# Masks and identities by VectorE from one table, and another order and other banks for the second keys and for units 2 and 3

## The chip, the cores and the metric

The kernel runs on one core of a Trainium2 chip. The metric is device time in microseconds (us); the kernel before took 285.91 us, the median of three runs (285.8 to 287.22). A core has five engines with a queue of instructions each: TensorE (PE in the profile, its weight loads PEld), VectorE (DVE), ScalarE (ACT), GpSimd (POOL) and SyncE (SP). 16 DMA engines move data between HBM and SBUF. Here the loads of q, k, v and of the weights, which also turn float32 into 16-bit types, are issued by GpSimd; stores and DMA transposes are issued by SyncE.

## What is computed

Attention in a sliding window (each position sees those at most 32 away), and after it two matrix products with a GELU in between.

```python
batch, n_heads, seq, head_dim = 8, 8, 576, 64
scores = q @ k^T / sqrt(64)                    # per head, 576 x 576
scores = where(|i - j| <= 32, scores, -1e9)
attn = softmax(scores)
x = (attn @ v) -> (4608, 512)                  # tokens x (heads * head_dim)
h = x @ w_in                                   # 512 -> 2048
g = h * sigmoid(1.702 * h)
out = g @ w_out                                # 2048 -> 512
```

Inputs and output are float32; inside, q, k, v and the weights of attention are bfloat16, x, g and the weights float16, sums float32 in PSUM.

## The kernel before

**Units and tiles.** The 4608 tokens are cut into 36 units of 128 queries, and four units make a tile of 512 tokens (nine tiles). Queries are taken 32 rows late, so that the keys that the 128 queries of a unit need are the unit's own 128 keys and the first 64 of the next: two blocks of 64 queries against 128 keys each, for each of eight heads.

**One unit of attention.** `scores(u, tag)` makes the transposed scores of both blocks in two PSUM banks (48 matmuls for two units) and then ScalarE takes the exponential of each bank into `p` (L255, two a unit). `band(u)` (L263, VectorE) multiplies `p` by a mask of zeros and ones. `values(u, tag)` multiplies `p` by the values. For the first block they are the unit's 128 rows (`ve`), for the second the 128 rows that begin 64 later (`vo`), which `odd_v(u, eng, parts)` puts together from two halves of `ve` (L209: one copy of 64x264 words for each part). Each value row has a one behind it, so the product also brings the sum of the weights. `norm(u)` (L292, L293, VectorE) divides by it into `x`. `x_T` and `x_T2` (L309, L321) transpose `x` of one or two units on TensorE against the identity `identh`, and a copy by VectorE or ScalarE (L67) writes it to `xT`, the form that the first product needs.

**The opening.** All orders are written out by hand, under a manual schedule: each engine runs its instructions in the order in which the code issues them, and waits on semaphores. `opening()` handles the first two tiles' attention and the first tile's layer 1:

- `load_first(c, part)` (L142) loads the first 576 keys and queries in two parts each: part 0 of k (320 rows) and q (256 rows), enough for units 0 and 1, and part 1 of each (256 rows), for units 2 and 3. `T_first(c, part, tags, engs)` (L167) transposes them with `ident` on TensorE, in two PSUM banks, each of which one engine of `engs` copies out. `load_four` and `T_four` (L177, L188) do the same for the second tile's 512 keys and queries.
- GpSimd issues, in this order: k0, q0, (identity), v of units 0 to 2, w_in columns 0 to 511 (`load_w1(0)`, L115), (mask), k1, q1, (four cuts of the mask), w_in columns 512 to 1023, v 3, half of v 4, w_in columns 1024 to 1535, the other half of v 4, `load_four` of k and q, w_in columns 1536 to 2047, v 5 and 6, w_out rows 0 to 511 (`load_w2(0)`, L119), v 7 and 8, three more loads of w_out, and then k, q and v of later units. Eight semaphores serve these loads in turn, so that the issue of a load also waits for the landing of the load eight places ahead of it.
- `setup_mask` (L102, L105) fills the four blocks (64 columns each) of the mask on GpSimd with ones and cuts triangles by affine_select; `cut_mask` (L111) zeroes four quarters of the two blocks that serve where a window ends at a batch's end. `ident` comes from the library's `make_identity` (masks.py), a memset and an affine_select on GpSimd; `identh` is its cast to float16 (L588, VectorE).
- `keep_busy(n, tag, cols)` issues n matmuls of zeros into an unused bank (the "fillers": `junk` in the profile).
- `layer1_plain(t, d, half, tag)` makes two of the 16 feature blocks of layer 1 for half a tile (256 tokens) in one bank with eight matmuls; ScalarE's GELU (L389) reads it. Blocks d = 0, 1 need w_in columns 0 to 511, d = 2, 3 the next 512, d = 4, 5 the third, d = 6, 7 the fourth. GELU and exponential are in different tables of ScalarE, with an ACT_TABLE_LOAD between them.
- `do(self.l2, n)` takes the next n matmuls of the first tile's layer 2. They use w_out rows in order: the first 8 need its first load, the next 8 the second, the next 8 the third.

**Later tiles.** From the second tile on, both products are done with seven products for eight (the sums `a`, `b`, `xs`, `gs` on VectorE), and `front`, `back` and `l1_group` mix attention of the next tile with them. None of that is touched.

**Banks.** PSUM has eight banks here: `t` is two of them, and A, C, B, E, LA, LB one each.

Of the kernel before, what the change touches and what calls it, by code (L numbers as in the profile page):

```python
# [15 lines left out]
F32 = mybir.dt.float32  # L16
# [4 lines left out]
ALU = mybir.AluOpType  # L21

SQ = 64
# [3 lines left out]
class _Kernel:  # L27
# [69 lines left out]
        self.spark = cst.tile([128, 1], F32, name="spark")  # L97

    def setup_mask(self):
        pool, m = self.nc.gpsimd, self.mask  # L100
        lo, hi = slice(0, 64), slice(64, 128)
        pool.memset(m, 1.0)  # L102
        for blks, rows, sign in ((slice(0, 2), lo, 1), (slice(0, 2), hi, -1), (slice(2, 4), lo, -1), (slice(2, 4), hi, 1)):
            ap = m[rows, blks, :]
            pool.affine_select(out=ap, in_=ap, compare_op=ALU.is_ge, fill=0.0, base=0,  # L105
                               pattern=[[0, 2], [-sign, SQ]], channel_multiplier=sign)

    def cut_mask(self):
        lo, hi = slice(0, 64), slice(64, 128)
        for b, rows, cols in ((0, hi, slice(0, 32)), (0, lo, slice(32, 64)), (2, lo, slice(0, 32)), (2, hi, slice(32, 64))):  # L110
            self.nc.gpsimd.memset(self.mask[rows, b, cols], 0.0)  # L111

    def load_w1(self, c, n=1):
        w = 512 * n
# [446 lines left out]
    def opening(self):  # L561

        nc, dve, act, pool = self.nc, self.nc.vector, self.nc.scalar, self.nc.gpsimd
        self.setup()
        dve.memset(self.idle, 0.0)
        dve.memset(self.spark, 0.0)
        for t in self.ve:
            dve.memset(t[:, :, self.D:], 1.0)
        self.load_first("k", 0)
        self.load_first("q", 0)  # L570
        make_identity(nc, self.ident)
        act.activation(self.spark, self.spark, AF.Exp)
        for u in (0, 1, 2):
            self.load_v(u)
        self.load_w1(0)
        self.setup_mask()
        self.load_first("k", 1)
        self.load_first("q", 1)
        self.cut_mask()
        self.load_w1(1)  # L580
        self.load_v(3)
        self.load_v(4, slice(0, 1))
        self.load_w1(2)
        self.load_v(4, slice(1, 2))
        self.load_four("k")
        self.load_four("q")
        self.load_w1(3)
        dve.tensor_copy(self.identh, self.ident)  # L588
        self.keep_busy(10, "E", 512)
        self.T_first("k", 0, "AC", (dve, act))  # L590
        self.keep_busy(2, "E", 512)
        self.T_first("q", 0, ("LA", "LB"), (dve, act))
        self.keep_busy(1, "E", 512)
        for u in (5, 6):
            self.load_v(u)
        self.load_w2(0)
        for u in (7, 8):
            self.load_v(u)
        for c in (1, 2, 3):
            self.load_w2(c)  # L600
        self.load_kq("k", 8)
        self.scores(0, "t")
        self.scores(1, "AC")
        self.odd_v(0, dve)
        self.odd_v(1, dve)
        self.keep_busy(4, "E", 512)
        self.band(0)
        self.values(0, "t")
        self.band(1)
        self.norm(0)  # L610
        self.values(1, "AC")
        self.norm(1)
        self.keep_busy(2, "E", 512)
        self.x_T(0, "LA", act)
        self.keep_busy(1, "E", 512)
        self.x_T(1, "LB", act)
        self.T_first("k", 1, "AC", (dve, dve))
        h, n, gelus = [], [0], []

        def l1(half, *ds):  # L620
            for d in ds:
                self.layer1_plain(0, d, half, h[n[0] % len(h)])
                n[0] += 1

        self.layer1_plain(0, 0, 0, "B", gelus)
        self.T_first("q", 1, ("LA", "LB"), (dve, act))
        self.layer1_plain(0, 1, 0, "E", gelus)
        self.odd_v(2, dve)
        self.odd_v(3, dve, (0,))
        h[:] = ["B", "E", "LA", "LB"]  # L630
        self.scores(2, "t")
        self.scores(3, "AC")
        self.layer1_plain(0, 2, 0, "LA", gelus)
        self.layer1_plain(0, 3, 0, "LB", gelus)
        self.do(gelus)
        self.band(2)
        self.odd_v(3, dve, (1,))
        self.band(3)
        self.values(2, "t")
        self.norm(2)  # L640
        self.values(3, "AC")
        self.norm(3)
        l1(0, 4)
        self.x_T2(2, "A", dve)
        l1(0, 5)
        dve.tensor_copy(self.k_first, self.kT[0][:, :, 0:64])
        dve.tensor_copy(self.v_first, self.ve[0][0:64])
        for u in (8, 9, 10, 11):
            self.fetch(u)
        l1(1, 0, 1)  # L650
        halo = self.kT[4]
        self.T_four("k", "AC", (dve, dve))
        dve.tensor_copy(self.kT[4][:, :, 0:64], halo)
        l1(1, 2, 3)
        self.T_four("q", "AC", (dve, act))
        l1(1, 4, 5)
        self.odd_v(4, dve)
        self.scores(4, "t")
        self.scores(5, "AC")
        self.odd_v(5, dve)  # L660
        for i in (3, 1, 2, 4):
            self.w1_sums((i,), 0)
        self.odd_v(6, dve)
        self.odd_v(7, dve, (0,))
        for d, tag in ((6, "B"), (7, "E")):
            self.layer1_plain(0, d, 0, tag, gelus)
        self.do(self.l2, 3)
        self.scores(6, "t")
        self.do(self.l2, 3)
        self.scores(7, "AC")  # L670
        self.do(gelus)
        self.do(self.l2, 2)
        self.band(4)
        self.band(5)
        self.odd_v(7, dve, (1,))
        self.band(6)
        self.values(4, "t")
        self.norm(4)
        self.band(7)
        self.values(5, "AC")  # L680
        self.norm(5)
        self.do(self.l2, 8)
        self.values(6, "t")
        self.norm(6)
        self.do(self.l2, 2)
        self.values(7, "AC")
        self.norm(7)
        h[:] = "BE"
        n[0] = 0
        self.w1_sums((3,), 1)  # L690
        l1(1, 6, 7)
        self.x_T2(4, "A", act)
        self.do(self.l2, 2)
        self.x_T2(6, "t", dve)
        self.do(self.l2, 4)
# [216 lines left out]
```

## Time and profile before

| | |
|---|---|
| median of three runs | 285.91 us (285.8 to 287.22) |
| profiled execution | 285.75 us, of which the span is 284.0 us |
| PE busy | 272.8 us (96%), 3684 matmuls |
| DVE busy | 217.2 us (76%), 501 instructions |
| ACT busy | 193.9 us (68%), 340 instructions |
| POOL busy | 126.9 us (45%), 192 instructions |
| chain that ended last | PE 82%, DMA 7%, DVE 5%, POOL 4% |
| queue of GpSimd's loads | 106000 packets, 18.42 MB |
| granted TensorE clock | 1.0 |

The span is cut from the first instruction to the last; the times of runs have 1.75 us around it. Busy times of matmuls overlap, as they are pipelined, so a busy share of PE near 100% doesn't say that it is at its peak. The chain is followed back from the last instruction, at each step to what released it. The opening, to which the change belongs, lasts until about 47 us of the span; in the first 42 us TensorE is busy in a smaller share than later.

### The profile page before, as it was taken

The numbers are of one execution on the slowest core, as the hardware profiler recorded it, in microseconds if no ns is written. First come the engines' busy times: TensorE is split into PE (matmuls) and PEld (weight loads), VectorE is DVE, ScalarE is ACT, GpSimd is POOL, SyncE is SP. The second block draws the span as 40 slices with busy tenths as digits, with TensorE's granted clock in tenths as the row PEclk, the third lists the DMA queues.
The fourth block names the chain that finished last, engine by engine and source line by source line (L and its number), as shares of the span: only waits on it lengthen the run. The fifth ranks groups of instructions, "written<-read, shape, count | busy, mean of one in ns | idle before, by whom it ended". The sixth has DMA issues, their size and how long they took to land.

```text
span 284.0 us, 8953 instructions
## 1 busy us (share of the span) xinstructions
PE 272.8 (96%) x3684; PEld 223.3 (79%) x3684; DVE 217.2 (76%) x501; ACT 193.9 (68%) x340; POOL 126.9 (45%) x192
## 2 busy tenths in 40 slices
PE   6787999999999998999999999999999999999995
PEld 2466847776778887888888888888888888888884
DVE  1754997898887877798879887878788878946731
ACT  2556684799886778667966796689658875568411
POOL 8975446898599726739083909340110000000000
PEclk9999999999999999999999999999999999999999
DMA  8999999999999999999999999995422030201024
GB/s 90 182 193 196 184 204 159 193 124 147 136 154 152 200 127 195 124 203 143 201 102 189 131 203 82 198 146 140 132 58 71 26 113 14 81 2 74 2 95 133
DMA packets 149610, 37.63 MB, mean 132 GB/s; under 512 B 138048, under 2 KB 145216, under 8 KB 149568
## 3 DMA queue, kind: packets, MB, share of 16 engines
q0 software_dynamic: 106000, 18.42, 95.0%
q1 hardware_dynamic: 43120, 18.10, 34.2%
q8 instruction: 29, 0.48, 0.7%
q10 hardware_dynamic: 448, 0.52, 0.6%
q14 instruction: 13, 0.11, 0.1%
HBM read 36.83 MB, written 9.44 MB: 163 GB/s over the span
## 4 chain that ended last, share of the span: by engine, by line
PE 82%; DMA 7%; DVE 5%; POOL 4%; issue 1%; ACT 0%; DVEq 0%; POOLq 0%
PE o L70 37%; PE h L70 36%; PE pv L70 4%; DMA w<-in_moe_w_in_dram 4%; DMA xT<-x 3%; PE sc L70 3%; POOL ve L198 1%; POOL kq L142 1%; DVE xs L353 1%; DVE vo L209 1%; PE tp L321 1%; PE tp L231 1%; DVE a L334 1%; PE tp L188 1%; POOL w L115 1%
## 5 line engine op out<-in xcount | busy, mean ns | idle before, releaser
L418 ACT ACTIVATE g<-h 128x512 f16<-128x512 f32 x128 | 72.2, 598 | 35.7 <-PE h L70 34.9
L70 PEld LDWEIGHTS <-g 128*128 128x128 f16 x576 | 54.4, 98 | 9.5
L70 PEld LDWEIGHTS <-a 128*128 128x128 f16 x512 | 49.1, 97 | 12.3 <-DVE xs L353 2.2
L70 PE MATMUL h<-xs,a 128*128 128x256 f16 x384 | 57.6, 272 | 0.9 <-DVE xs L353 0.7
L70 PE MATMUL o<-w,g 128*128 128x256 f16 (+1 forms) x320 | 55.5, 294 | 0.0
L70 PEld LDWEIGHTS <-w 128*128 128x128 f16 x512 | 48.9, 98 | 8.4 <-DMA w<-in_moe_w_in_dram 1.7
L70 PE MATMUL h<-xT,w 128*128 128x256 f16 x384 | 54.0, 273 | 1.4 <-DMA w<-in_moe_w_in_dram 1.4
L209 POOL COPY vo<-ve 64x264 int32<-64x264 int32 x55 | 25.5, 463 | 61.3 <-PE pv L70 59.0
L70 PEld LDWEIGHTS <-gs 128*128 128x128 f16 x384 | 36.8, 98 | 4.7
L255 ACT ACTIVATE p<-sc 128x512 bf16<-128x512 f32 x72 | 36.9, 620 | 2.6 <-PE sc L70 2.5
L70 PE MATMUL o<-b,gs 128*128 128x256 f16 x256 | 37.6, 273 | 0.0
L70 PE MATMUL o<-b,g 128*128 128x256 f16 x256 | 37.5, 273 | 0.0
L198 POOL DMA_DIRECT2D ve<-in_v_dram x40 | 34.4, 865 | 6.2 <-DMA qst<-in_q_dram 2.8
L431 DVE TENSOR_TENSOR h<-h,s 128x512 f32<-128x512 f32 x32 | 22.3, 698 | 17.8 <-PE h L70 17.5
L131 POOL DMA_DIRECT2D qst<-in_q_dram x35 | 28.1, 804 | 3.5 <-DMA w<-in_moe_w_out_dram 2.8
L67 ACT COPY h<-h 128x512 f32<-128x512 f32 x32 | 18.9, 589 | 15.5 <-PE h L70 15.1
L293 DVE TENSOR_TENSOR x<-pv,rec 128x256 f16<-128x256 f32 (+1 forms) x53 | 27.6, 520 | 1.8
L131 POOL DMA_DIRECT2D kst<-in_k_dram x31 | 26.4, 855 | 5.0 <-DMA ve<-in_v_dram 2.6
L437 DVE TENSOR_TENSOR h<-h,s 128x512 f32<-128x512 f32 x32 | 22.4, 700 | 4.6 <-PE h L70 3.9
L263 DVE TENSOR_TENSOR p<-p,mask 128x1024 bf16<-128x1024 bf16 x36 | 25.0, 698 | 0.8 <-ACT p L255 0.6
L67 ACT COPY s<-h 128x512 f32<-128x512 f32 x32 | 19.2, 599 | 2.0 <-PE h L70 0.7
L70 PE MATMUL h<-xs,w 128*128 128x256 f16 x128 | 19.2, 273 | 0.0
(83 smaller groups left out, 343.7 us busy)
## 6 DMA issues: line engine op xcount, KB each, us to landing
out_dram<-o_sb SPq DMA_DIRECT2D x33, 256.0 KB, 4.6
ve<-in_v_dram POOLq DMA_DIRECT2D x32, 128.0 KB, 6.6
kst<-in_k_dram POOLq DMA_DIRECT2D x25, 128.0 KB, 6.6
qst<-in_q_dram POOLq DMA_DIRECT2D x21, 128.0 KB, 6.1
w<-in_moe_w_in_dram POOLq DMA_DIRECT2D x4, 512.0 KB, 8.9
w<-in_moe_w_out_dram POOLq DMA_DIRECT2D x4, 512.0 KB, 12.6
qst<-in_q_dram POOLq DMA_DIRECT2D x7, 96.0 KB, 6.4
kq<-in_q_dram POOLq DMA_DIRECT2D x2, 256.0 KB, 5.9
```

Of the source, the lines that this page charges most:

```text
L67: (eng.copy if eng is self.nc.scalar else eng.tensor_copy)(out, in_)
L70: self.nc.tensor.matmul(out, lhsT, rhs, start=start, stop=stop, skip_group_check=True)
L115: self.nc.gpsimd.dma_start(self.w1[:, :, c * 512:c * 512 + w], self.w_in[:, c * 512:c * 512 + w].rearrange("(k p) f -> p k f", p=128))
L131: self.nc.gpsimd.dma_start(t[off:off + n], src[b, :, s:s + n, :].rearrange("h s d -> s h d"))
L198: self.nc.gpsimd.dma_start(t[off:off + n, :, :self.D], self.v[b, :, s:s + n, :].rearrange("h s d -> s h d"))
L209: eng.tensor_copy(*((words(vo[64:128]), words(self.ve[u % 9][64:128])), (words(vo[0:64]), words(nxt)))[i])
L255: self.nc.scalar.activation(p[:, eo].rearrange("k h s -> k (h s)"), sc[eo], AF.Exp, scale=self.scale)
L263: (eng or self.nc.vector).tensor_mul(pv, pv, msk.to_broadcast([128, 8, 2, SQ]))
L293: dve.tensor_mul(x[:, 4 * at:4 * (at + n), :].rearrange("p (b h) d -> p b h d", b=n), acc[:, :, :, :D], r.to_broadcast([128, n, 4, D]))
L418: act.activation(g[:, f, 256 * half:256 * half + 256], bank.rearrange("p (i n) -> p i n", i=2), AF.Gelu_apprx_sigmoid)
L431: dve.tensor_add(e, b, s7)
L437: dve.tensor_add(c, b, s7)
```

## The change

The mask and both identities are made in another way. GpSimd writes one table D of 128x128 float32 with D[p, j] = p - j (iota). VectorE compares it with zero: D = 0 is `ident`, which it casts to `identh`; D >= 0 and D <= 0 on the two 64-row halves are the mask's triangles. The four cuts are VectorE's memsets. `setup_mask` and `cut_mask` are called right behind the first two loads, and GpSimd's queue goes from the table straight to v of unit 0. The order of the loads among each other stays as it was.

The second part of the keys (`T_first("k", 1)`) is transposed ahead of `x_T(0)` and `x_T(1)` and not behind them, with two fillers less, in LA and LB in place of A and C; its copies are by ScalarE and VectorE and not both by VectorE. `x_T(0)` uses bank t, `x_T(1)` LA, and the second queries B and E. Scores of units 2 and 3 follow at once (t, B and E), and the first two blocks of layer 1 come behind them, in A and C. On VectorE `band(2)` stands ahead of the second half of `odd_v(2)`, and on TensorE `values(2)` stands ahead of the third block of layer 1 and `values(3)` ahead of the fourth. The transposes of x of units 2 and 3 (`x_T2(2)`) come ahead of layer 1's fifth block and not behind it, in bank t. The banks of the blocks behind them follow from that.

```diff
@@ -97,18 +97,23 @@
         self.spark = cst.tile([128, 1], F32, name="spark")
 
     def setup_mask(self):
-        pool, m = self.nc.gpsimd, self.mask
-        lo, hi = slice(0, 64), slice(64, 128)
-        pool.memset(m, 1.0)
-        for blks, rows, sign in ((slice(0, 2), lo, 1), (slice(0, 2), hi, -1), (slice(2, 4), lo, -1), (slice(2, 4), hi, 1)):
-            ap = m[rows, blks, :]
-            pool.affine_select(out=ap, in_=ap, compare_op=ALU.is_ge, fill=0.0, base=0,
-                               pattern=[[0, 2], [-sign, SQ]], channel_multiplier=sign)
+
+        D = self.work.tile([128, 128], F32, name="gap", tag="s7", bufs=2)
+        self.nc.gpsimd.iota(D, pattern=[[-1, 128]], base=0, channel_multiplier=1,
+                            allow_small_or_imprecise_dtypes=True)
+        dve = self.nc.vector
+        dve.tensor_single_scalar(self.ident, D, 0.0, op=ALU.is_equal)
+        dve.tensor_copy(self.identh, self.ident)
+        for r in (slice(0, 64), slice(64, 128)):
+            d = D[r, r].rearrange("p (b s) -> p b s", b=1).to_broadcast([64, 2, SQ])
+            up = int(r.start > 0)
+            for blk, op in ((2 * up, ALU.is_ge), (2 - 2 * up, ALU.is_le)):
+                dve.tensor_single_scalar(self.mask[r, blk:blk + 2, :], d, 0.0, op=op)
 
     def cut_mask(self):
         lo, hi = slice(0, 64), slice(64, 128)
         for b, rows, cols in ((0, hi, slice(0, 32)), (0, lo, slice(32, 64)), (2, lo, slice(0, 32)), (2, hi, slice(32, 64))):
-            self.nc.gpsimd.memset(self.mask[rows, b, cols], 0.0)
+            self.nc.vector.memset(self.mask[rows, b, cols], 0.0)
 
     def load_w1(self, c, n=1):
         w = 512 * n
@@ -568,15 +573,14 @@
             dve.memset(t[:, :, self.D:], 1.0)
         self.load_first("k", 0)
         self.load_first("q", 0)
-        make_identity(nc, self.ident)
+        self.setup_mask()
+        self.cut_mask()
         act.activation(self.spark, self.spark, AF.Exp)
         for u in (0, 1, 2):
             self.load_v(u)
         self.load_w1(0)
-        self.setup_mask()
         self.load_first("k", 1)
         self.load_first("q", 1)
-        self.cut_mask()
         self.load_w1(1)
         self.load_v(3)
         self.load_v(4, slice(0, 1))
@@ -585,7 +589,6 @@
         self.load_four("k")
         self.load_four("q")
         self.load_w1(3)
-        dve.tensor_copy(self.identh, self.ident)
         self.keep_busy(10, "E", 512)
         self.T_first("k", 0, "AC", (dve, act))
         self.keep_busy(2, "E", 512)
@@ -610,11 +613,12 @@
         self.norm(0)
         self.values(1, "AC")
         self.norm(1)
-        self.keep_busy(2, "E", 512)
-        self.x_T(0, "LA", act)
+        self.T_first("k", 1, ("LA", "LB"), (act, dve))
         self.keep_busy(1, "E", 512)
-        self.x_T(1, "LB", act)
-        self.T_first("k", 1, "AC", (dve, dve))
+        self.x_T(0, "t", act)
+        self.keep_busy(1, "E", 512)
+        self.x_T(1, "LA", act)
+        self.T_first("q", 1, "BE", (dve, act))
         h, n, gelus = [], [0], []
 
         def l1(half, *ds):
@@ -622,26 +626,25 @@
                 self.layer1_plain(0, d, half, h[n[0] % len(h)])
                 n[0] += 1
 
-        self.layer1_plain(0, 0, 0, "B", gelus)
-        self.T_first("q", 1, ("LA", "LB"), (dve, act))
-        self.layer1_plain(0, 1, 0, "E", gelus)
-        self.odd_v(2, dve)
-        self.odd_v(3, dve, (0,))
-        h[:] = ["B", "E", "LA", "LB"]
         self.scores(2, "t")
-        self.scores(3, "AC")
+        self.scores(3, "BE")
+        self.layer1_plain(0, 0, 0, "A", gelus)
+        self.layer1_plain(0, 1, 0, "C", gelus)
+        self.odd_v(2, dve, (0,))
+        self.band(2)
+        self.odd_v(2, dve, (1,))
+        self.odd_v(3, dve)
+        self.values(2, "t")
         self.layer1_plain(0, 2, 0, "LA", gelus)
+        self.band(3)
+        self.norm(2)
+        self.values(3, "BE")
         self.layer1_plain(0, 3, 0, "LB", gelus)
         self.do(gelus)
-        self.band(2)
-        self.odd_v(3, dve, (1,))
-        self.band(3)
-        self.values(2, "t")
-        self.norm(2)
-        self.values(3, "AC")
         self.norm(3)
+        h[:] = ["A", "C", "LA", "LB", "B", "E"]
+        self.x_T2(2, "t", dve)
         l1(0, 4)
-        self.x_T2(2, "A", dve)
         l1(0, 5)
         dve.tensor_copy(self.k_first, self.kT[0][:, :, 0:64])
         dve.tensor_copy(self.v_first, self.ve[0][0:64])
@@ -653,6 +656,7 @@
         dve.tensor_copy(self.kT[4][:, :, 0:64], halo)
         l1(1, 2, 3)
         self.T_four("q", "AC", (dve, act))
+        h[:], n[0] = ["LA", "LB"], 0
         l1(1, 4, 5)
         self.odd_v(4, dve)
         self.scores(4, "t")
```

## The prediction

> **What bounds the kernel now.** I read four views. The first is the chain that ended last, in order of time (start us, length us, what); the edit touches only the first 30 us.
>
> ```profile
> 8.72 1.73 POOL kq L142 x2
> ...
> 13.27 10.13 DMA w<-in_moe_w_in_dram
> 23.44 1.05 PE h L70 x8
> 24.94 2.71 PE h L70 x24
> ...
> 38.17 1.30 DVE p L263 x2
> ...
> 39.97 1.83 PE o L70 x8
> 41.80 0.38 PE pv L70 x16
> 42.20 0.59 PE o L70 x2
> ```
>
> Up to 13.27 it names GpSimd's issues, then for 10.13 us a load of w_in (columns 1024 to 1535, call it C2), then TensorE, then VectorE's chain from 31.2 to 39.5, then TensorE. So the first question is whether C2 came late because it was issued late. The DMA view of the first 60 us (each cell 1.5 us) and three issues with KB and us from issue to landing answer that: first keys, C2, then the third w_out load (call it W2).
>
> ```profile
> DMA  0199999999999999999999999999999999999999
> GB/s 0 6 106 187 168 154 196 211 173 187 205 181 184 208 186 197 190 199 203 199 164 199 189 171 218 194 208 203 196 162 151 150 153 153 157 158 239 252 153 69
> ```
>
> ```profile
> kq<-in_k_dram POOLq DMA_DIRECT2D x1, 256.0 KB, 6.0
> w<-in_moe_w_in_dram POOLq DMA_DIRECT2D x1, 512.0 KB, 10.1
> w<-in_moe_w_out_dram POOLq DMA_DIRECT2D x1, 512.0 KB, 12.9
> ```
>
> The engines are never idle after 3 us. Ahead of and with C2, 3200 KB are queued; at the cells' 150 to 210 GB/s that is 16 to 22 us from 2.8 us on, and C2 landed at 13.27 + 10.1 = 23.4. It was waiting in a queue. The timeline (start, length) shows who waits:
>
> ```profile
> 12.41 0.60 PE L70 MATMUL junk<-idle 128*128 128x512 bf16 x2
> 14.75 0.64 PE L167 MATMUL tp<-ident,kq 128*64 128x128 bf16 x16 [0.50 <-DMA kq<-in_k_dram]
> 16.30 0.64 PE L167 MATMUL tp<-ident,kq 128*64 128x128 bf16 x16
> 17.85 0.70 PE L70 MATMUL sc<-kq 64*64 64x64 bf16 x48
> 23.44 1.05 PE L70 MATMUL h<-xT,w 128*128 128x256 f16 x8 [1.24 <-DMA w<-in_moe_w_in_dram]
> 24.33 0.61 PE L321 MATMUL tp<-identh,x 128*128 128x128 f16 x8
> 42.11 0.19 PEld L70 LDWEIGHTS <-g 128*128 128x128 f16 x2
> 42.20 0.59 PE L70 MATMUL o<-w,g 128*128 128x512 f16 x2
> ```
>
> TensorE idles 1.24 us for C2 at 23.44. The last pair matters most: at 42.11 the weights of the output product are loaded, at 42.20 its matmul starts; two us earlier (39.90) both started together. That matmul needs W2, issued at 29.28 (the timeline), landed 12.9 later, at 42.2. A second DMA bound stands there, hidden by 0.1 us.
>
> **Masks and identities.** GpSimd loses 0.22 + 0.29 (identity), 0.36 + 1.33 + 0.59 (mask): 2.79 us, and gains one table of indices. That row isn't there; the nearest are the memset (0.22) and the select (0.29) of the same shape; in 4-byte words up to twice that, so 0.2 to 0.6, and I take 0.3. The issues of the second keys and queries and all behind them come 1.9 (keys) to 2.5 us earlier. Nothing lands earlier, by the queue above: the issues only wait longer, and later ones wait for earlier landings anyway (1.56 and 2.07 us of idle ahead of w loads in GpSimd's timeline). Cost 0; if the queue were not the bound, up to -2.3 (a rival). VectorE gains the identity, its cast (already there, 0.20), four mask compares and four memsets: nearest rows 0.20 for 128x128, 0.28 to 0.66 for a 64x264 copy, 0.07 for its small memsets. 0.2 + 0.2 + 4 x 0.2 + 4 x 0.07 = 1.5, at most 3.4, from 3.6 us on. It sits idle until 6.60 (2.75 us, waiting for the first key transposes), so cover is there for 3.0; the identity is ready at 3.9 and first used at 6.01. Cost 0, 0.4 at the worst.
>
> **Second keys moved forward.** On TensorE the transposes of k part 1 now stand ahead of those of x0 and x1. They wait for their load, so TensorE idles from 12.4 to 14.75 (in before 14.25 to 14.75) with x0, x1 and fillers queued behind. Those take 2 x 0.23 (filler, two starts at 12.41 end 0.60 later, 0.38 each) + 2 x 0.23 (four starts 0.056 apart) = 0.9 and fit between 15.2 (the key transposes' last start) and 16.3, when the q part 1 transposes began because of their load. ScalarE's four copies between 15.2 and 17.58 (about 0.5 apart) fit as well; its copy of q then starts at 16.99 as before. Nobody else waits: x0, x1 are needed by layer 1 at 18 us. Cost 0; with one copy late, +0.5.
>
> **Scores 2 and 3 ahead of layer 1.** In before, eight layer-1 matmuls (16.88, 1.05 us) held TensorE when q's copies ended (DVE 17.46, ACT 17.58). Without them scores start at about 17.55, 0.3 earlier, and so does the second exponential (ends 19.43 in before, 19.13 then). VectorE follows: band(2) 0.61, three half copies of odd values 3 x 0.31, band(3) 0.61, norm(2) 0.20 + 0.61, norm(3) 1.17 (start to start, timeline at 20.2 to 23.6): 19.15 + 4.13 = 23.3. The load of values 3 ended a wait at 19.58 in before; now its copy follows band(2), at 19.76, and waits no more. TensorE has 32 layer-1 matmuls (0.11 apart, 3.5), two value products (0.45 each) in the same 18.05 to 22.6, so VectorE ends last. The transposes of x2 and x3 then end near 23.45, when C2 has just landed; in before they came behind its first eight matmuls. That takes 8 x 0.056 = 0.45 off TensorE's path, and 0.05 to 0.19 of a wait for their copy: k's second tile starts near 27.05 in place of 27.57. -0.5. Other end: every copy of values at 0.66 (the worst row, beside a GpSimd issue) is 3 x 0.37 = 1.1 later, +0.6. I take -0.5: 14 of the 16 up to 40 us are below 0.55.
>
> **What is late next.** From 31.2 to 39.5 VectorE's chain moves along by the 0.5; its loads of values (landed 31.95 to 37.04) still come in time. Then the product at 42.20 needs W2 at 42.2, and W2 does not move, since its queue has the same bytes in the same order. So at most 0.1 us gets past it. A loss of up to 0.6 would lose 0.1 there and pass with 0.5. Behind 42.2 TensorE is busy 17.77 of 17.80 us to 60, in an unchanged order.
>
> **Sum.** 0 (masks) - 0.5 (order) + 0.45 (given back at W2) = -0.05; ends -0.1 and +0.9. The profiled execution took 285.75 us (span 284.0, 1.75 around it); it becomes 285.7. The median of the three runs is 0.16 above it, so I predict 285.8.
>
> **Rival 1, slower: TensorE loses its clock in the new gap.** The first fillers ran at a slow rate: weight loads at 1.68, 2.10, 2.53 us, 0.43 apart, while the fillers at 12.41 are 0.22 apart. So there is a slow state at rest. In before, products and fillers never pause for over 1.9 us after 5 us (13.49 to 15.32); now, between 12.4 and 17.55, there are two fillers and transposes. It decides when the clock falls before layer 1 at 18 us and stays for half of its 32 matmuls or more: each then takes 0.11 more, +1.7 to +3.5, less 0.5 spare and 0.1: 286.9 to 288.6, likeliest 287.7. Against it: the gap alone is 2.35 us, and the clock reads 1.00 through all of before. The Trainium skill's page "TensorE: Matmul & The Clock Gate" (Why this matters for your kernels) wants no gap over about 3 us, by which the clock would stay; its Part 4 adds that transposes don't count as busy, which makes the gap 2.8 us up to the first filler at 15.2. No run here shows either yet. Chance 0.18, of which 0.15 beyond 0.5%.
>
> **Rival 2, faster: the issues were the bound.** The chain names GpSimd up to 13.27. If an engine ran dry between issues, C2 and W2 come up to 2.3 us earlier: 283.5. Against: no cell of the DMA row falls below 9. Chance 0.09, of which 0.07 beyond 0.5%.
>
> **Rival 3, slower: VectorE's new work and GpSimd's issues hinder each other.** Two value copies beside issues took 0.66 and 0.63 where 0.29 is usual. If the v issues at 3.6 to 6.2 are held for the length of eight VectorE operations, the stream runs dry once: +0.5 to +2, 286.3 to 287.8. Against: the v issue beside the cast took 0.901, its fellows 0.888 and 0.893. The Trainium skill, "SBUF — State Buffer" (SBUF: two separate sides), says a VectorE operation that takes the shared port blocks GpSimd's writing of descriptors; these three rows show no sign of it. Chance 0.07, 0.05 beyond.
>
> **Chances.** The forecast has 0.66, all within 0.5% (1.43 us, about what a measurement of this kernel can tell from no change). With the rivals' small ends: faster 0.07, same 0.73, slower 0.20. The range goes from 284.7 (a third of rival 2, and spread between runs) to 287.7 (rival 1's likeliest); it leaves out rival 2's larger part (0.07), rival 1 above (0.08) and rival 3's end (0.02).
>
> **What would show it.** Right: second keys and C2 land at 14.7 and 23.4 though issued about 2 us earlier; scores 2 near 17.55; the x2, x3 transposes ahead of C2's matmuls; k's second tile near 27.05; the W2 product again at 42.2. Wrong: layer-1 matmuls 0.2 apart or a granted clock below 1 between 14 and 22 us (rival 1); W2's matmul well before 42 (rival 2); lower GB/s in cells before 10 us (rival 3); value copies or exponentials later than listed, with the product past 42.5.

## Result and the profile after

The change made the kernel slower by a little: 287.34 us, the median of 15 runs (285.84 to 288.68), against 285.8 us for the kernel before in the same comparison; the ratio is 1.004, with a 95% interval of 1.0025 to 1.0055. This ratio, like all those below, compares the runs in the faster of two states in which a kernel runs here, and so is not the quotient of the two medians (1.0054). The profiled execution took 288.68 us, its span is 286.9 us and its mean granted clock 0.994 (before: 285.75, 284.0 and 1.0). It is the slowest of the 15, 1.34 us above their median, so it shows more loss than the kernel usually has. Times of one kernel spread by one to three us. Two things that differ between executions of the same instructions are seen below: where the steps of TensorE's clock fall, and when a group of DMA transposes at 107 to 113 us gets through. Whether they make up the whole spread isn't shown.

The first view is the timeline of TensorE in the kernel after (start us, length us, engine, line, operation, shapes, count, and in brackets the idle time before and who ended it):

```profile
14.62 0.71 PE L172 MATMUL tp<-ident,kq 128*64 128x128 bf16 x16 [2.06 <-DMA kq<-in_k_dram]
15.67 0.63 PE L314 MATMUL tp<-identh,x 128*128 128x128 f16 x4
17.09 1.07 PE L172 MATMUL tp<-ident,kq 128*64 128x128 bf16 x16
18.53 0.89 PE L70 MATMUL sc<-kq 64*64 64x64 bf16 x48 [0.37 <-DVE kq L67]
19.35 1.92 PE L70 MATMUL h<-xT,w 128*128 128x256 f16 x16
24.26 0.89 PE L326 MATMUL tp<-identh,x 128*128 128x128 f16 x8
28.57 1.11 PE L193 MATMUL tp<-ident,o_sb 128*64 128x128 bf16 x32
42.91 0.61 PE L70 MATMUL o<-w,g 128*128 128x512 f16 x2
```

TensorE idles 2.06 us ahead of the second keys, nearly as foreseen (2.35). What follows was not foreseen: the second queries' transposes take 1.07 us where they took 0.64, and scores 2 and 3 0.89 where they took 0.70. Scores 2 start at 18.53 (forecast 17.55), the second tile of keys at 28.57 (forecast 27.05), and the product that needs W2 at 42.91 (forecast 42.2). The table of engines by stretch (start and end, length, busy us of each engine with its count, then the granted clock; the last two columns, of the DMA, aren't used here) says why:

```profile
core 0: us, PE busy (x) PEld busy (x) DVE busy (x) ACT busy (x) POOL busy (x), PEclk, DMA share, GB/s
8.23:11.64 3.41, 1.78 (x57) 1.06 (x59) 2.90 (x7) 2.35 (x5) 3.41 (x6) 1.00 1.61 192
11.64:15.05 3.41, 1.20 (x48) 0.97 (x46) 2.32 (x7) 0.00 (x0) 1.63 (x3) 1.00 1.74 185
15.05:18.47 3.42, 3.11 (x34) 1.95 (x28) 1.38 (x2) 2.02 (x4) 1.35 (x2) 0.50 1.64 187
18.47:21.88 3.41, 3.09 (x78) 2.49 (x80) 1.82 (x5) 2.97 (x6) 2.55 (x3) 1.00 1.45 197
```

The clock's own record, kept with the trace, has it full from 4.81 us on, half for one stretch of 3.41 us, and full again. The stretch before the half one is the one with the gap: TensorE was busy 1.20 us of 3.41.

In the DMA view, k1, C2 and W2 (KB, us from issue to landing) read:

```profile
kq<-in_k_dram POOLq DMA_DIRECT2D x1, 256.0 KB, 8.0
w<-in_moe_w_in_dram POOLq DMA_DIRECT2D x1, 512.0 KB, 11.8
w<-in_moe_w_out_dram POOLq DMA_DIRECT2D x1, 512.0 KB, 12.8
```

They were issued at 6.62, 10.65 and 29.64 (before 8.67, 13.27 and 29.28) and landed at 14.6, 22.4 and 42.4 (before 14.7, 23.4 and 42.2). So 2.05 us of earlier issue brought the keys 0.1 us. C2 came one us earlier, which the prediction did not foresee. That the earlier issue did it isn't shown: in two kernels below whose issues stayed at the old times (before without its fillers, and the masks with GpSimd's old work) it landed at 22.37 and 22.52 too, and nothing in the change waits for it.

A second loss lies far behind the change. In the profiled execution after, ScalarE's exponentials and GELUs run 0.88 us later than before's up to 106 us, and 2.58 us later at 112. The waits of TensorE from 97 to 118 us (total, times, longest), and then the chain there:

```profile
PE sc L70 <- DMA kT<-kst: 1.2, 1, 1.2
PE h L70 <- DVE xs L358: 0.9, 1, 0.9
```

```profile
103.87 8.23 DMA xT<-x
...
113.80 1.05 PE h L70 x8
```

The same two views of before, the one wait and the transpose in the chain:

```profile
PE h L70 <- DVE xs L353: 0.7, 1, 0.7
100.79 8.72 DMA xT<-x
```

Before had only the second of the two waits there, and its chain goes through a DMA transpose of x at this place as well; in the change that one starts 3.08 us later.

### The profile page after: what moved, and what is told of

The parts are those of the page before. It is cut to its first block, busy times and chain, and to the rows that moved or that the text cites. A ratio compares the mean times of both kernels' runs of the same rounds, so it can differ in the third digit from the quotient of the medians.

```text
span 286.9 us, 8946 instructions
## 1 busy us (share of the span) xinstructions
PE 274.1 (96%) x3681; PEld 224.6 (78%) x3683; DVE 219.2 (76%) x509; ACT 194.7 (68%) x341; POOL 124.7 (43%) x182
## 4 chain that ended last, share of the span: by engine, by line
PE 83%; DVE 7%; DMA 6%; POOL 2%; issue 1%; ACT 1%; POOLq 0%; DVEq 0%
PE o L70 37%; PE h L70 36%; PE pv L70 4%; PE sc L70 3%; DMA xT<-x 3%; DMA kq<-in_k_dram 3%; DVE vo L214 1%; DVE a L339 1%; DVE xs L358 1%; DVE p L268 1%; POOL ve L203 1%; PE tp L326 1%; PE tp L236 1%; DVE x L298 1%; POOL kq L147 1%
## 5 line engine op out<-in xcount | busy, mean ns | idle before, releaser
L436 DVE TENSOR_TENSOR h<-h,s 128x512 f32<-128x512 f32 x32 | 22.4, 699 | 17.8 <-PE h L70 17.6
L442 DVE TENSOR_TENSOR h<-h,s 128x512 f32<-128x512 f32 x32 | 22.4, 699 | 4.6 <-PE h L70 4.0
```

The lines of the kernel that those rows point to most:

```text
L436: dve.tensor_add(e, b, s7)
L442: dve.tensor_add(c, b, s7)
```

## Experiments

Three theories were stated at first. A: the clock that TensorE loses because of the gap is the loss. B: the new order is slower by itself. C: the loss arises later, in DMA transposes behind the opening. "M", later on, is the suspicion that the new masks cost something. In three comparisons the kernel before took 286.23 (first four kernels), 286.47 (next four) and 286.11 us (last four).

**Fillers in the gap.**

```diff
+        self.keep_busy(9, "E", 512)
         self.T_first("k", 1, ("LA", "LB"), (act, dve))
```

> The changed kernel with nine fillers (0.22 us each, 2.0 us) ahead of the second keys' transposes, in the gap that ran from 12.4 to 14.6. Theory A (the clock drops to half because of the gap, and that is the loss): mean granted clock back to 1.00, layer-1 matmuls 0.11 apart everywhere, x2 and x3's transposes end near 23.5, and the time equals that of before within 0.3% (285.5 to 286.5). Theory B (the order itself is slower, by its waits on VectorE): clock 1.00 too, but the time stays near 287.3. Theory C (the loss arises in the later DMA transposes and has nothing to do with the opening): time stays near 287, with the opening as early as before.

286.1 us, ratio 1.0009 (0.999 to 1.0028). The clock was at 0.998 or more in 11 of 12 runs, where the change without fillers had 0.987 to 0.994 in 14 of 15. One line that adds work takes the loss away, so A holds for the median. The products of this kernel are in the order of the change, so B, as the cause of the loss, falls. The two intervals just touch here (1.0028 and 1.0025); with four fillers, below, they are apart.

**The order alone**, with the masks of before (`setup_mask`, `cut_mask` and `make_identity` at their old places).

> The changed order and banks, with masks and identities made by GpSimd as before. Theory A: the clock falls as in the changed kernel (mean 0.99) and the time is the changed kernel's within 0.2%, 286.8 to 287.8. A theory by which VectorE's mask work or the earlier issues cost the time expects before's 285.8 here.

287.74 us, ratio 1.0061 (1.0037 to 1.0084), with a clock of 0.987 to 0.994 in nine of ten runs. The slow part of the change is the order with its gap. The tenth run is the profiled one, whose clock came up only at 10.56 us and then stayed; it shows the opening as forecast (scores 2 at 17.40, k's second tile at 27.10).

**The masks alone**, with the old order.

> Masks and identities by VectorE from the table, with the order and banks of before. Theory A and the prediction's queue: loads issued about 2 us earlier land at the same times (second keys 14.7, columns 1024 to 1535 of w_in near 23), clock 1.00, time 285.8 within 0.2%. If the earlier issues help: 283.5 to 285.2. If VectorE's work beside GpSimd's issues hurts: over 286.5.

286.85 us, ratio 1.0028 (1.0006 to 1.005), and that with the clock at 0.994 to 1.0. This was not expected by A, and it falls where the expectation for VectorE hindering GpSimd's issues had it (over 286.5). The trace shows no sign of that mechanism, though: the issues of v take as long as before. In its profiled execution, the slowest of the 12, k1 landed at 15.34 (before 14.7). The time is lost at two places: the W2 product starts 0.36 us later than before's, and another 0.5 us goes at 107 to 113 us.

**The kernel before without the three fillers around x0 and x1.**

```diff
-        self.keep_busy(2, "E", 512)
         self.x_T(0, "LA", act)
-        self.keep_busy(1, "E", 512)
         self.x_T(1, "LB", act)
```

> The kernel before without the three fillers between the second value product and the second keys' transposes; nothing else is moved. Theory A with transposes not counting as work: the clock falls as in the changed kernel (mean 0.99), and the time rises by 0.7 to 1.7 us. Theory A with only an idle TensorE counting (its gaps here stay below 1.2 us): clock 1.00 and 285.8.

286.27 us, ratio 1.0013 (0.9995 to 1.0032). The clock fell in 11 of 12 runs. So before's fillers were holding its clock. The time rose less than the 0.7 to 1.7 us that were expected, by 0.4 us with an interval that reaches to nothing: a lost stretch there costs less than in the change. The profiled execution, one of three runs at 0.988 (two lost stretches), by stretch:

```profile
9.92:13.33 3.41, 1.71 (x38) 0.90 (x36) 3.20 (x9) 1.35 (x4) 3.32 (x9) 1.00 1.48 195
13.33:16.75 3.42, 2.95 (x26) 1.94 (x27) 1.82 (x5) 1.14 (x2) 3.35 (x5) 0.50 1.51 197
```

TensorE was busy for half of the first stretch, and the clock is half in the next.

**The order alone, with fillers** (nine, as above).

> The new order with the masks of before, and nine fillers of 512 columns ahead of the second key transposes, so that TensorE has no idle gap there. Theory A (the lost clock is the whole loss): the granted clock stays at 1.0 and the time is that of the same kernel with the new masks, 0.1% over before or less, 286.1 where before takes 286.2. Theory M (the masks cost 0.28% by themselves, as the run of the masks alone measured, and the order alone is worth the -0.5 us that was predicted): ratio about 0.998, 285.6. Theory B (the order itself is slower): 1.003 or more with the clock at 1.0.

The clock was at 0.997 or more in 11 of 12 runs, but the median is 287.15 us, ratio 1.0023 (1.0001 to 1.0046): neither A nor M foresaw that, and the interval holds the 1.003 of B. Five of its runs lie at 287.4 to 289.1 us with the clock at 0.997 or more; no trace shows why, so this run doesn't tell whether the order itself costs 0.2% with the old masks. The profiled execution (286.94 us) reaches the point forecast for the opening, and then gives it up. Its timeline of TensorE:

```profile
17.35 0.70 PE L70 MATMUL sc<-kq 64*64 64x64 bf16 x48 [0.57 <-DVE kq L67]
27.05 1.11 PE L188 MATMUL tp<-ident,o_sb 128*64 128x128 bf16 x32
42.02 0.59 PE L70 MATMUL o<-w,g 128*128 128x512 f16 x2 [0.30 <-DMA w<-in_moe_w_out_dram]
```

Scores 2 start 0.20 us ahead of the forecast, k's second tile at 27.05, the very number of it, and ScalarE's work is 0.52 us ahead of before from 32 to 41 us. Then TensorE waits 0.30 us for W2, and 0.19 us are left at 49. They go at 107 to 113 (0.2 lost) and at 210 to 215 us (0.4 lost).

**Transposes instead of an idle gap.**

```diff
+        tp = self.bank("E", [128, 4, 128], BF16, "tp")
+        for i in range(38):
+            nc.tensor.transpose(tp[:, i % 4, :], self.idle[:, 0:128], self.ident)
         self.T_first("k", 1, ("LA", "LB"), (act, dve))
```

> The changed kernel with 38 transposes of a zero tile (about 2.1 us) instead of an idle TensorE ahead of the second key transposes; the transposes write a bank that nobody reads. If any work of TensorE keeps its clock up (the profiled runs so far: the clock fell after stretches of 3.41 us with TensorE busy 0.35 and 0.50 of the time, transposes counted, and stayed after 0.52, 0.53 and 0.63): clock 0.998 to 1.0 and the time of the run with nine fillers, ratio 1.000 to 1.002. If transposes do not count as work for the clock: granted clock 0.987 to 0.994 in nearly all runs and 1.004, as the change without fillers.

The clock stayed at 0.998 or more in 11 of 12 runs; 286.46 us, ratio 1.0025 (0.9996 to 1.0053), a little outside the expected 1.000 to 1.002. Four runs at 287.8 to 289.3 widen the interval, three of them with the clock held, so the time settles nothing here and the clock does. By stretch:

```profile
10.90:14.31 3.41, 2.64 (x65) 2.48 (x66) 3.06 (x8) 0.21 (x1) 2.18 (x3) 1.00 1.65 187
14.31:17.73 3.42, 2.85 (x73) 2.15 (x74) 1.64 (x3) 2.19 (x4) 1.54 (x2) 1.00 1.47 196
```

Without the transposes, TensorE's products fill 0.26 and 0.29 of these two stretches, less than in the stretch without fillers in before (0.39, with transposes 0.50) after which the clock fell. So transposes count as work for the clock.

**Four fillers instead of nine.**

> The changed kernel with four fillers instead of nine. The idle gap shrinks from 2.2 to about 1.35 us, which lifts the least busy stretch of 3.41 us from 0.35 to about 0.60. Theory A with a limit near one half: the clock stays at 0.998 to 1.0 and the ratio is 1.000 to 1.002. If the clock wants a gap near nothing: 0.994 and 1.004, the order of 0.9 us slower than with nine fillers.

286.14 us, ratio 0.9994 (0.998 to 1.0008), clock at 0.998 or 1.0 in all 12 runs, though TensorE still idles 1.32 us ahead of the second keys. Its stretch with the transposes shows once more that these count, since products alone fill only 0.23 of it, as in the stretch of the change after which the clock fell:

```profile
13.64:17.05 3.41, 2.15 (x42) 1.60 (x42) 1.23 (x3) 1.51 (x3) 1.35 (x2) 1.00 1.46 200
```

About 0.85 us of work that nobody reads is worth 0.46% (1.3 us) against the change without it, by the two ratios to before.

**The masks alone, with GpSimd's old work kept** on a second mask that nobody reads, so that its issues are at the old times.

> The masks and identities by VectorE in the old order of work, and GpSimd still makes a second mask that nobody reads, at the old places, so that its issues of the second keys and of all behind them stay nearly at the times of before. If the 0.28% of the masks alone came from the earlier issues: ratio 1.000, within 0.1%. If it came from VectorE's work or from anything else that went with the masks: 1.003 again.

286.69 us, ratio 1.0018 (0.9999 to 1.0037): between the two expectations, and it settles neither. In its profiled execution the whole loss is there at 49 us: the W2 product starts 0.60 us late.

**The first two W2 products later**, on the version with four fillers.

```diff
         self.norm(6)
-        self.do(self.l2, 2)
         self.values(7, "AC")
...
         self.x_T2(4, "A", act)
-        self.do(self.l2, 2)
+        self.do(self.l2, 4)
```

> The changed kernel with four fillers, and its first two products with W2 moved behind the last layer-1 work of the opening, so that W2 may land some 3 us later. If W2 is what takes the gain back (the run with four fillers was 0.20 us ahead of before at 38 us and 0.01 at 49): 0.2 us ahead at 49 us and to the end of the profiled run, ratio 0.998 to 0.999. If the 0.2 is lost to something else at 41 to 49 us: 0.0 at 49 and 0.9994 again.

286.18 us, ratio 1.0014 (0.999 to 1.0037); no gain. ScalarE's work is 0.35 us ahead of before at 45 us, and 0.08 behind at 49. The chain shows VectorE's `norm` in W2's place: its last multiplication ends at 42.46, and the values of unit 7 start at 42.51. W2 landed at 41.8 in this execution, so two limits lie 0.6 us apart; the two products (0.44 us) had been filling part of the wait for the later one, and now take their time behind it.

**The late transposes of x by TensorE**, on the version with four fillers: `x_T2(14, "t", act)` within the second group's products, in place of two DMA transposes.

```diff
                 self.values(u + n - 1, "t")
                 self.norm(u + n - 1)
-                self.x_T(u + n - 1)
+                if n == 1:
+                    self.x_T(u + n - 1)
...
                 if t == 2 and n in (1, 3) and i == 7:
                     self.values(u + n, "t")
                     self.norm(u + n)
-                    self.x_T(u + n)
+                    if n == 1:
+                        self.x_T(u + n)
+                if t == 2 and n == 3 and i == 2:
+                    self.x_T2(u + n - 1, "t", self.nc.scalar)
```

> The changed kernel with four fillers, and the last two transposes of x for the fourth tile (units 14 and 15, about 98 to 112 us) made by TensorE with one copy by ScalarE instead of by two DMA transposes. Theory C (the second step at 107 to 113 us, +1.7 us in the profiled run of the change, +0.5 with the masks alone, -0.8 in another, comes from when these DMA transposes get through): no step of more than 0.2 us upwards at 106 to 112, some 0.5 us down, times closer together, ratio 0.996 to 0.998. If it comes from the DMA transposes of the keys beside them: TensorE still waits there in some runs, ratio 0.999 to 1.001 and a spread as before.

285.78 us (285.37 to 286.79), ratio 0.9991 (0.9974 to 1.0008). The chain at the place of the second loss:

```profile
101.10 0.45 PE tp L326 x8
...
106.54 0.63 PE sc L70 x32
107.17 1.57 PE o L70 x12
108.73 0.44 PE h L70 x4
```

There is no DMA and no wait in it. The transposes, at 101 us, cost 0.39 us, and 0.95 us come back by 118. Both waits, that for x and that for the keys' transposes, are gone with two DMA transposes fewer. One execution would not show it, since the one with transposes in the gap has no wait there either; but all three profiled executions with this edit (this one and the next two) have none, and ten of the eleven without it have one. So C is right about the place of the second loss. The median gains no more than the measurement can tell from nothing, and the times did not come closer together as expected: 1.42 us from lowest to highest, where the version with four fillers has 1.44.

**Both edits on the version with four fillers, and both on the kernel before.**

> Both edits together: 0.2 us and 0.5 us if both theories hold, ratio 0.995 to 0.998, 0.7 us below before. If the W2 edit brings nothing, as the one with the transposes alone.

> The kernel before with the same two edits, and none of the change. If the changed order is worth its 0.2 to 0.5 us once the clock is held and W2 is out of the way, this one is 0.1 to 0.2% slower than the version with both edits on the change: ratio 0.997 to 0.999, with a clock below 1 in about a quarter of the runs, as before. If it is as fast as that version, the change brought nothing even then.

285.97 us, ratio 0.9991 (0.9973 to 1.0008), and 286.15 us, ratio 1.0009 (0.9987 to 1.003). The second is 0.18% slower than the first, as expected, with three of its 12 runs at a clock of 0.994, also as expected, and the first is as fast as the version with the transposes alone, as expected if the W2 edit brings nothing. But the intervals cover these differences, and neither is at the 0.995 to 0.998 and 0.997 to 0.999 of the theories or beats the kernel before by more than the uncertainty. The second one's profiled execution is worth more than its time. It lost its clock at another place, that of before's 1.24 us wait for C2:

```profile
19.87:23.28 3.41, 1.58 (x39) 1.04 (x38) 3.28 (x10) 3.38 (x6) 1.56 (x2) 1.00 1.50 195
23.28:26.69 3.41, 3.41 (x21) 2.63 (x22) 0.90 (x3) 0.93 (x2) 2.33 (x3) 0.50 1.45 195
```

The kernel before has the same weak spot in its profiled execution, TensorE busy 1.82 us of 3.41:

```profile
21.31:24.72 3.41, 1.82 (x38) 1.52 (x33) 2.22 (x7) 2.66 (x6) 1.25 (x3) 1.00 1.54 193
```

Of its 103 runs in the three comparisons 19 show a clock below 0.995, though not where they lost it. In the first two comparisons the median of such runs lies 0.9 and 0.6 us above that of the others. The new order fills that wait with the transposes of x2 and x3.

How far ScalarE's exponentials and GELUs stand from before's in the profiled executions (us, minus is earlier), beside the start of the first W2 product (the kernels that move this product are left out):

| kernel | W2 product | at 38 us | at 49 | at 100 | at 112 | at 275 |
|---|---|---|---|---|---|---|
| the change | 42.91 | +1.00 | +0.73 | +0.88 | +2.58 | +2.72 |
| nine fillers | 42.06 | -0.20 | -0.15 | -0.14 | -0.13 | +0.01 |
| order alone | 41.95 | -0.47 | -0.26 | -0.25 | -0.33 | +0.03 |
| masks alone | 42.56 | -0.25 | +0.35 | +0.36 | +0.88 | +0.90 |
| before, no fillers | 43.20 | +1.29 | +1.06 | +1.07 | +1.25 | +1.26 |
| order alone, fillers | 42.02 | -0.52 | -0.19 | -0.18 | +0.05 | +0.41 |
| transposes in the gap | 42.04 | -0.22 | -0.07 | -0.06 | -0.85 | -0.70 |
| four fillers | 42.20 | -0.20 | -0.01 | -0.01 | -0.11 | +0.04 |
| masks, old issues | 42.80 | -0.01 | +0.59 | +0.60 | +0.64 | +0.63 |
| x by TensorE | 41.87 | -0.30 | -0.34 | -0.34 | -0.66 | -0.90 |

The first three columns of numbers tell the story of the opening (before's W2 product starts at 42.20): whatever was gained by 38 us, the shift at 49 is that of the W2 product, to 0.02 us in eight of the ten rows and to 0.09 in the other two (before without fillers, transposes in the gap). In seven rows that product started within 0.05 us of W2's landing. In the change it came 0.5 us after W2's landing at 42.4: VectorE released the values of unit 5 only at 40.20, and eight products and the values of unit 6 stood between these and the W2 product. The step at 112 does not follow from being late: before without fillers is 1.07 us late at 100 us, later than the change, and its step is 0.2 us.

## Why the prediction was wrong, step by step

**The step that failed is "Second keys moved forward".** It counted the idle time (12.4 to 14.75; measured 12.56 to 14.62) and who was queued behind it, and put its cost at 0, because everything fitted into the time. It priced the gap in work and not in clock. (The description of the change is off by one there: before has three fillers around x0 and x1 and the change two, so it has one less, and neither of the two stands in the gap.) The gap left 1.20 us of work in a stretch of 3.41, the next stretch ran at half clock, and the transposes of the second queries and the scores took 0.6 us more; with the waits between them, scores 2 came 1.0 us after the forecast. At 38 us the change is 1.2 us behind the same kernel with four fillers, and between the ratios of the two to before lies 0.46% (1.3 us); for nine fillers it is 0.31% (0.9 us).

**Rival 1 is what happened; it had been given a chance of 0.18.** Its range (286.9 to 288.6, likeliest 287.7) holds the 287.34. Two of the reasons against it misled. The first, "the gap alone is 2.35 us", compares the length of a gap with a limit, but what counts is how busy a whole stretch is. The second, "the clock reads 1.00 through all of before", was read as room to spare, when the least busy stretch in the opening of before had 1.82 us of 3.41. That the price fits is partly luck. Its likeliest case was about 2 us over the forecast, on the path of the layer-1 matmuls; holding the clock was worth 0.9 to 1.3 us, and by another path: the layer-1 matmuls ran at full speed (16 in 1.92 us), since the half clock ended at 18.47, and what it had slowed was what they wait behind.

The Trainium skill's page "TensorE: Matmul & The Clock Gate" was cited for both sides there. Its figure for a gap (Why this matters for your kernels, about 3 us) would have kept the clock; 2.06 us lost it. Its Part 4, by which transposes do not count, made the gap longer; the runs with transposes and with four fillers show that they count. Its Part 1 has the rule that fits: a window of 3413 ns that runs on its own. The stretches here are 3.41 us long.

**"Masks and identities", cost 0: right where it was worked out.** The table took 0.26 us on GpSimd (estimate 0.3), VectorE's part ran from 3.36 to 5.53, within the bounds of 1.5 to 3.4 us and ahead of its first copy at 6.39. The loads did not come 2 us earlier with their issues, and the time did not fall, so rival 2 is out. The v issues took 0.89 us each beside VectorE's work, so the mechanism of rival 3 isn't seen. What stays open is why the masks alone measured 0.28% slower, and 0.18% with the old issues, while the change with fillers, which has the same masks, did not; in the profiled executions of the two the loss is seen at the W2 product, which waits for W2, and in the first of them at 107 to 113 us as well.

**"Scores 2 and 3 ahead of layer 1", -0.5: right in kind**, once the clock was held, and in size with the old masks alone: 0.52 in the order alone with fillers, where k1 landed at 14.54. With the new masks too, it landed at 14.85 in the versions with four and nine fillers, and 0.2 was left (0.3 in that with x by TensorE, where it landed at 14.67). The slack that the step before counted on (0.9 us of work from 15.2 to 16.3) was nearly all used, so that the landing of k1 now seems to set the scores.

**"What is late next", 0.45 given back at W2: right in kind.** 0.33 was given back in the order alone with fillers, 0.19 with four fillers. The prediction took W2 as fixed at 42.2; it landed between 41.8 and 42.8, and where the product waited for it, this is passed on to the end of the opening in full.

**"Sum", -0.05.** With the clock held, 285.98 and 286.01 us in the profiled executions with nine and four fillers, against 285.7 forecast. Behind 42 us the sum had only "an unchanged order". That left out the DMA transposes at 107 to 113 us: the step there is between -0.8 (transposes in the gap) and +1.7 us (the change) in executions whose instructions there are the same.

## What to carry to other kernels

When an edit moves TensorE's work, cut the opening into stretches of the clock's length and add up TensorE's busy time in each, before and after: a stretch near one half is a risk, wherever its pieces lie. A few matmuls of zeros in front of a wait are cheap and can be worth more than the reordering that made the wait. A gain that is worked out up to one wait needs the next two: here W2 and VectorE stood 0.6 us apart, and DMA transposes 60 us later moved by more than all of it.

## What the runs showed of the hardware

- The granted clock changes only at the ends of stretches of 3.41 us, whose start differs from run to run: in all 14 profiled executions the clock's record has only periods of a whole number of them, up to the last (10.24 us is three, 279.89 us 82). It fell after stretches with TensorE busy 1.20, 1.58 and 1.71 us (0.35, 0.46, 0.50) and stayed after 1.78 and 1.82 (0.52, 0.53), transposes counted. These are all cases below 0.54 between the first full grant and 35 us in the profiled executions here, so the limit is near one half. The rise from the half clock did not follow the same number: it stayed half after a stretch of 0.86 in the kernel before without fillers.
- How often a kernel loses its clock fits this only in part. Wherever stretches of 3.41 us are laid over the profiled execution of the change, one of them has TensorE busy less than 0.46 of it, and 14 of 15 runs lost the clock. Over that of before, about three positions in ten give a stretch below one half, and 19 of 103 runs lost it; with nine fillers or transposes in the gap none do, and one run of 12 each did. It does not fit two kernels. By before's trace without its three fillers, three in ten positions should lose the clock there, and 11 of 12 runs did; by the trace of the order alone, in which the clock came up late, none should, and nine of ten did. So one execution is too little for this estimate, or the share is not the whole rule.
- One of a load's 16 shares can land far behind the others: in the change 15 shares of k1 were there at 13.68 and the last at 14.58; in the order alone without fillers the last came at 13.80. The trace of the change has a 16 KB fetch of instructions at 12.13 us, 0.97 us long, and 28 more, 5 to 15 us apart. In the order alone that fetch starts at 13.34; in the other 13 profiled executions it starts between 11.7 and 13.0, and k1's last share lands between 14.5 and 15.3. So the fetch goes with the late share; that it is the cause was not tried.
- In the version with the transposes of x by TensorE, the last copy to the output buffer starts at 279.90 us, 0.91 earlier than before's, and the span is only 0.3 us shorter: what follows that copy, the last store, took 0.6 us longer.
